# A planner that counts GpSimd's whole-tile operations as holding VectorE up

## The chip, the core and the metric

The kernel runs on one core of a Trainium2 chip. The metric is device time in microseconds of one execution; lower is better. The engines named below are TensorE (PE in the profile, with PEld for its weight loads), VectorE (DVE), ScalarE (ACT), GpSimd (POOL) and SyncE (SP), which issues every DMA of this kernel.

## What is computed

Three blocks in a row, all float32 (the inputs arrive as float64 where the code decodes them): a two-way attention between 512 tokens and 32 state rows for 8 batches and 8 heads, a feed-forward block with a SoLU and a layer norm, and a feed-forward block with a squared ReLU.

```python
scores = scale * np.matmul(x, state.transpose(0, 1, 3, 2))
a = softmax(scores);   xread = np.matmul(a, state)
a2 = softmax(scale * np.matmul(state, x.transpose(0, 1, 3, 2)));   sread = np.matmul(a2, x)
x = concatenate([xread, sread], axis=2)          # 4352 rows of 512
h = x @ w_in
solu = h * softmax(h);   ln = (solu - mu) / np.sqrt(var + 1e-06) * g_ln
x = ln @ w_out                                   # w_in 512x1024, w_out 1024x512
r = np.maximum(x @ w2_in, 0.0)
out = (r * r) @ w2_out                           # w2_in 512x2048, w2_out 2048x512
```

(`softmax` stands for the maximum, exponential and sum that the reference writes out.)

## The kernel before

Large products are made of three passes over a high half and a low half of each operand. ScalarE copies a tile into its high half, and a subtraction makes the low half; that subtraction can run on VectorE, or on GpSimd where both operands are in SBUF.

Phase one goes over 8 batches and a last group of 256 state rows. For each batch it computes scores (`scores`), transposes them (`emit_sT`, tile `sTp`), makes softmax weights `a_sb` and transposes these (`emit_aT`, tile `aTp`), multiplies state and `w_in` (`emit_sw`, tile `sw`), forms four tiles of `h` (`emit_l1`, PSUM tile `hps`), and takes each through `solu_rest`: maximum (L557, L574), exponential (L581), product (L586), square (L592), four small GpSimd operations for the root (L600 to L607), normalisation of `u` (L610). Then `emit_lnT` transposes `u` (tile `lnTp`), splits it into `lt` (ScalarE L653, VectorE L656), and `emit_l2` multiplies by `wo` into `y` (L682), which is stored in DRAM. The `h` of batch b+1 and the scores of batch b+2 are interleaved with the eight steps of batch b.

Weights are decoded on chip (`decode`: ScalarE L300, VectorE L303 and L306). `wi` and `wo` are decoded at the start. The weights of phase two's first product are decoded, combined and split in the background of batches 1 to 6 (`early_w2`, tiles `dec` and `w2s`, stored to DRAM as `w_d`), and those of its second product at the turn to phase two (`load_wb`, tiles `wb`). Phase two then goes over the nine groups with a seven-product scheme (`emit_l3`, L1005) and the last product (`emit_l4`, L1076).

TensorE's order is written out by hand. The order on all other engines is made by a planner in Python, class `Flow`, as the program is built; the chip then runs each engine's list in the order given, with semaphores. The planner keeps one clock `now`, and a time `free` for each of VectorE (V), ScalarE (A), GpSimd (P) and the DMA queue (D). Work off TensorE is written as generators that yield steps: a dictionary of engines with planned costs, a time from which the step is ready, and a function that emits it. Costs that matter here:

- the low half of a decoded weight tile (`split_w` and `keep` in `early_w2`): 1.25 on P or 0.69 on V;
- the softmax product in `rest` of `emit_sT` (L435): 1.2 on P or 0.69 on V;
- the normalisation of `u` (L610): 1.7 on P or 0.75 on V;
- the root of `solu_rest`: 2.4 on P, no choice.

`poll` goes over the open tasks by urgency (the due time found in a first planning round, less the costs still to come), takes a step if its chosen engine is free within 0.1 of `now`, and chooses the engine by the least of free time + cost + `SPARE`, where `SPARE` is 0.7 for V. `pe` moves the clock on by TensorE's planned times and marks due times. The program is planned twice: the second round takes due times and costs from the first.

```python
eng = min(engs, key=lambda e: max(self.free[e], self.now) + engs[e] + self.SPARE[e])
if self.free[eng] > self.now + self.EARLY:
    continue
```

Of the kernel before, what the change touches and what calls it, by code (L numbers as in the profile page):

```python
# [28 lines left out]
class Flow:  # L29
# [12 lines left out]

    SPARE = {"V": 0.7, "A": 0.0, "P": 0.0, "D": 0.0}
    NEVER = 1e9

    def __init__(self, plan=None):

        self.plan, self.made = plan, []
        self.now = 0.0
        self.end = 0.0  # L50
        self.warm = self.WARM_UP
        self.free = {"V": 0.0, "A": 0.0, "P": 0.0, "D": 0.0}
        self.tasks = []

    def run(self, eng, cost, ready, emit):
        start = max(self.free[eng], ready, self.now)
        self.free[eng] = start + cost
        emit(eng)
        return start + cost + (2.0 if eng == "D" else self.HOP)

    def spawn(self, gen, slack=8.0):


        task = {"gen": gen, "req": None, "done": None, "slack": slack, "costs": [],
                "by": self.NEVER, "n": len(self.made)}
        self.made.append(task)
# [36 lines left out]
    def latest(self, task):  # L103

        if self.plan:
            by, costs = self.plan[task["n"]]
            if by < self.NEVER:
                return by - sum(costs[len(task["costs"]):])
# [45 lines left out]
def attn_solu_relu2_kernel(  # L154
# [645 lines left out]
    def load_y(j):  # L800
# [7 lines left out]
        def few():  # L808
            for k in range(2):
                t, f = yield from raw_y(k)  # L810
                yield from split_y(j, k, t, f)
                give("raw")

        def gen():
            a1, f1 = yield from raw_y(0)
            a2, f2 = yield from raw_y(1)
            a11, a21, a12, a22 = (a[:, :, i:i + Q] for a in (a1, a2) for i in (0, Q))
            tmp = []
            yield from split_y(j, "A11", a11, f1)
            for _ in range(3):  # L820
                yield take("dec")
                tmp.append(dec_p.tile([P, 512], F32, tag="dec", name="sy", bufs=3).rearrange(
                    "p (k t) -> p k t", k=2
                ))
                if len(tmp) == 1:
                    s1 = tmp[0]
                    f2 = yield {"V": 0.69}, f2, lambda e: nc.vector.tensor_tensor(
                        out=s1, in0=a21, in1=a22, op=ALU.add
                    )
                elif len(tmp) == 2:  # L830
                    s2 = tmp[1]
                    f = yield {"V": 0.69}, f2 - fl.HOP, sub(s2, s1, a11)
                    yield from split_y(j, "S2", s2, f)
                    yield from split_y(j, "A12", a12, f2)
                else:
                    s3 = tmp[2]
                    f = yield {"V": 0.69}, f2, sub(s3, a11, a21)
                    yield from split_y(j, "S3", s3, f)
                    give("dec")
            yield from split_y(j, "S1", s1, f2)  # L840
            give("dec")
            f = yield {"V": 0.69}, f2, sub(s2, a12, s2)
            yield from split_y(j, "S4", s2, f)
            give("dec")
            yield from split_y(j, "A22", a22, f2)
            give("raw")
            give("raw")

        for name in range(2) if j == B else [a for _, a, _ in PRODUCTS]:
            done["y", j, name] = {"by": fl.NEVER, "done": None}  # L850
        done["y", j] = fl.spawn(few() if j == B else gen())
# [32 lines left out]
    for t in range(T):  # L884
        run(emit_l1(0, t, t % 2 == 0))
        if t % 2:
            emit_e(0, t // 2)
            if t < T - 1:
                exp_t(0, t // 2 + 1)
# [13 lines left out]
    for b in range(B):  # L903
# [5 lines left out]
        for k in range(K1):  # L909
# [28 lines left out]
            if b == B - 1:  # L938
                if k in (0, 2):
                    after[3].append(lambda: run(emit_l1s(k // 2)))  # L940
                if k == 3:
                    fl.need([done["w2_d", m] for m in range(M2)])
                    phase2_right()
                    load_y(0)
                if k in (4, 6):
                    load_wa(0, k // 2 - 2)
                if k in (5, 6, 7):
                    load_wb(wb_order[k - 5])
# [5 lines left out]
            if k in l1_at and nxt:  # L954
                run(emit_l1(b + 1, l1_at.index(k)))
# [203 lines left out]
```

## Time and profile before

| what | value |
|---|---|
| median of three runs | 1150.2 us (1149.54 to 1151.52) |
| profiled execution, its own time | 1151.89 us |
| its span, first to last instruction | 1149.7 us |
| TensorE busy | 1116.0 us (97%) |
| VectorE busy | 727.9 us (63%) |
| ScalarE busy | 457.5 us (40%) |
| GpSimd busy | 155.4 us (14%) |

The span leaves out what lies ahead of the first and behind the last instruction. Busy shares are means over stages that differ: GpSimd works in phase one and at the turn to phase two only, so a reader goes by stretches of the span and not by the shares of the whole. A group of instructions is named by line, engine, operation and tile; L256 is a helper's line that many subtractions share, and there the tile tells them apart.

### The profile page before, as it was taken

What the parts mean: (1) busy time and instruction counts of PE and PEld (TensorE: products, weight loads), DVE (VectorE), ACT (ScalarE), POOL (GpSimd) and SP (SyncE); (2) the same over time, 40 slices, a digit from 0 to 9 for tenths busy, and PEclk for the clock granted to TensorE, in tenths of its full rate; (3) what the DMA queues carried; (4) which work ended last, traced back from release to release, by engine and by line L of the source; (5) the groups of instructions that cost most, each with busy time, mean ns of one, the idle gap of its engine ahead of it and who ended that gap; (6) DMA issues with size and microseconds to landing.
All of it is one profiled execution on the core that took longest, in us unless ns stands there. A gap on an engine that the chain in (4) does not pass through costs nothing.

```text
span 1149.7 us, 17914 instructions
## 1 busy us (share of the span) xinstructions
PE 1116.0 (97%) x7144; PEld 943.9 (82%) x7144; DVE 727.9 (63%) x1429; ACT 457.5 (40%) x848; POOL 155.4 (14%) x209
## 2 busy tenths in 40 slices
PE   4899999999999999999999999999999999999998
PEld 1377777777777689999989999999899989989987
DVE  6776878778777468885655745745754655655522
ACT  5866767677766464331211221311211211221121
POOL 1532323334134122300000000000000000000000
PEclk8999999999999999999999999999999999999999
DMA  9322163462443729855555555556555565465353
GB/s 351 146 80 98 57 227 131 152 216 85 166 147 111 292 85 337 318 180 198 221 196 198 197 214 205 190 202 223 196 185 212 192 217 190 179 229 191 129 192 111
DMA packets 42691, 214.02 MB, mean 186 GB/s; under 512 B 4976, under 2 KB 14192, under 8 KB 31344
## 3 DMA queue, kind: packets, MB, share of 16 engines
q1 hardware_dynamic: 42608, 212.88, 51.6%
q8 instruction: 56, 0.92, 0.3%
q14 instruction: 27, 0.22, 0.1%
HBM read 178.26 MB, written 34.60 MB: 185 GB/s over the span
## 4 chain that ended last, share of the span: by engine, by line
PE 67%; DVE 1%; ACT 0%; DMA 0%; issue 0%; POOL 0%; SPq 0%; DVEq 0%; ACTq 0%
PE o L1076 32%; PE h L1005 30%; PE y L682 3%; PE hps L621 1%; DMA raw<-w_in 0%; PE lnTp L647 0%; DVE u L586 0%; DVE lt L656 0%; POOL wb L256 0%; DVE hm L557 0%; ACT e L581 0%; DVE u L610 0%; ACT u L250 0%; ACT lt L653 0%; DVE yt L256 0%
## 5 line engine op out<-in xcount | busy, mean ns | idle before, releaser
L1076 PE MATMUL o<-wb,g 128*128 128x512 f32 x1632 | 383.4, 390 | 0.0
L1005 PEld LDWEIGHTS h<-yt,wa 128*128 128x128 f32 x2880 | 354.9, 192 | 5.5
L1005 PE MATMUL h<-yt,wa 128*128 128x256 f32 x2880 | 356.6, 283 | 0.0
L1076 PEld LDWEIGHTS o<-wb,g 128*128 128x128 f32 x1632 | 301.9, 188 | 59.8
L682 PE MATMUL y<-lt,wo 128*128 128x512 f32 (+1 forms) x864 | 218.3, 394 | 3.1 <-ACT lt L653 2.4
L985 DVE TENSOR_TENSOR u<-u,h 128x256 f32<-128x256 f32 x192 | 80.3, 418 | 177.3 <-ACT u L250 151.6
L682 PEld LDWEIGHTS y<-lt,wo 128*128 128x128 f32 x864 | 148.9, 189 | 39.8 <-issue 5.9
L250 ACT CAST g<-r 128x512 fp32r<-128x512 f32 x136 | 82.5, 622 | 222.1 <-DVE r L993 222.1
L985 DVE TENSOR_TENSOR r<-u,h 128x256 f32<-128x256 f32 x256 | 100.7, 417 | 24.8 <-PE h L1005 24.7
L993 DVE SCALAR_TENSOR_TENSOR r<-r 128x512 f32<-128x512 f32 x136 | 89.6, 697 | 29.3 <-ACT r L1028 29.3
L621 PE MATMUL hps<-sw,aT 128*128 128x512 f32 x368 | 98.4, 416 | 1.0 <-ACT s_sb L356 1.0
L256 DVE TENSOR_TENSOR g<-r,g 128x512 fp32r<-128x512 f32 x136 | 88.3, 688 | 14.5 <-ACT g L250 11.2
L250 ACT COPY u<-h 128x256 f32<-128x256 f32 x64 | 23.8, 372 | 183.0 <-PE h L1005 183.0
L621 PEld LDWEIGHTS hps<-sw,aT 128*128 128x128 f32 x368 | 69.7, 192 | 24.8 <-issue 6.2
L656 DVE SCALAR_TENSOR_TENSOR lt<-lnTp,g_sb,lt 128x512 fp32r<-128x512 f32 (+1 forms) x72 | 51.4, 714 | 26.2 <-ACT lt L653 25.5
L557 DVE TENSOR_REDUCE hm<-hps 128x1 f32<-128x512 f32 x68 | 45.9, 687 | 26.6 <-PE hps L621 21.0
L250 ACT COPY u<-hps 128x512 f32<-128x512 f32 x68 | 39.1, 583 | 41.9 <-DVE hm L557 40.5
L653 ACT ACTIVATE lt<-lnTp,g_sb 128x512 fp32r<-128x512 f32 (+1 forms) x72 | 48.2, 671 | 5.4 <-PE lnTp L647 5.3
L586 DVE SCALAR_TENSOR_TENSOR u<-u,e 128x1024 f32<-128x1024 f32 x34 | 44.4, 1307 | 8.4 <-ACT e L581 8.2
L592 ACT ACTIVATE e<-u,nmu 128x1024 f32<-128x1024 f32 x34 | 39.2, 1153 | 12.7 <-DVE nmu L589 12.7
L647 PE MATMUL lnTp<-ident,u 128*128 128x128 f32 x272 | 41.6, 274 | 1.5 <-DVE a_sb L256 1.4
L581 ACT ACTIVATE e<-u,nmx 128x1024 f32<-128x1024 f32 x34 | 39.2, 1153 | 6.8 <-DVE nmx L574 5.8
(92 smaller groups left out, 838.4 us busy)
## 6 DMA issues: line engine op xcount, KB each, us to landing
wa<-w_d SPq DMA_DIRECT2D x64, 1792.0 KB, 7.2
w_d<-w2s SPq DMA_DIRECT2D x32, 512.0 KB, 2.9
raw<-w_out SPq DMA_DIRECT2D x24, 512.0 KB, 5.5
out<-osb SPq DMA_DIRECT2D x34, 256.0 KB, 4.9
xT<-x_t SPq DMA_DIRECT2D x8, 1024.0 KB, 5.2
xn<-x_n SPq DMA_DIRECT2D x8, 1024.0 KB, 6.7
y_d<-ys SPq DMA_DIRECT2D x16, 512.0 KB, 4.1
raw<-w_in SPq DMA_DIRECT2D x16, 512.0 KB, 5.9
```

Source lines behind the costliest of these rows:

```text
L250: nc.scalar.copy(out=out, in_=in_)
L256: return lambda e: eng_of[e].tensor_tensor(out=out, in0=in0, in1=in1, op=ALU.subtract)
L557: one({"V": 0.68}, lambda e, c=c, ps=ps: nc.vector.tensor_reduce(out=m2[:, c:c + 1], in_=ps, axis=AX.X, op=ALU.max)),
L586: nc.vector.scalar_tensor_tensor(out=u, in0=u, scalar=1.0, in1=e_, op0=ALU.mult, op1=ALU.mult, accum_out=us)
L621: nc.tensor.matmul(out=ps, lhsT=lhsT(i, k), rhs=rhs(j, k)[:, cs], start=(k == 0 and n == 0), stop=(k == n_k - 1 and n == len(passes) - 1),)
L653: f = yield {"A": 0.1 + nt * 0.143}, f, lambda e: nc.scalar.activation(out=o[:, 0], in_=pf, func=AF.Copy, scale=gk)
L656: f = yield {"V": 0.1 + nt * 0.155}, f, lambda e: nc.vector.scalar_tensor_tensor(out=o[:, 1], in0=pf, scalar=gk, in1=o[:, 0].bitcast(F32), ...
L682: nc.tensor.matmul(out=ps, lhsT=wo[k][:, w, c * P:(c + 1) * P], rhs=o[:, a], start=(k == 0 and i == 0), stop=(k == K1 - 1 and i == 2),)
L985: return then({"V": 0.42}, lambda e: nc.vector.tensor_tensor(out=out, in0=in0, in1=in1, op=op), *tasks)
L993: f = yield {"V": 0.69}, max(t["done"] for t in tasks), lambda e: nc.vector.scalar_tensor_tensor(out=r, in0=r, scalar=0.0, in1=r, op0=ALU. ...
L1005: nc.tensor.matmul(out=ps, lhsT=w[:, y, k], rhs=a[:, x, k], start=(first and k == 0 and i == 0), stop=(last and k == 1 and i == 2),)
L1076: nc.tensor.matmul(out=ops[j][t], lhsT=g[:, a, h, t * P:(t + 1) * P], rhs=wb[m + h * M2][:, w, :], start=(m == 0 and h == 1 and i == 0), s ...
```

## The change

`run`, which every planned step goes through, books VectorE as well when a step goes to GpSimd at a planned cost under 2.0: VectorE's free time becomes the later of itself and the step's start, plus 0.7 of the cost. The root (2.4) is left out by the bound. Nothing else is edited; the planner's lists of instructions follow from it.

```diff
     SPARE = {"V": 0.7, "A": 0.0, "P": 0.0, "D": 0.0}
     NEVER = 1e9
+    HELD = 0.7
...
     def run(self, eng, cost, ready, emit):
         start = max(self.free[eng], ready, self.now)
         self.free[eng] = start + cost
+        if eng == "P" and cost < 2.0:
+
+            self.free["V"] = max(self.free["V"], start) + self.HELD * cost
         emit(eng)
         return start + cost + (2.0 if eng == "D" else self.HOP)
```

## Rows read from the trace of the kernel before

**Rows 1.** Four stretches: from:to length, busy (instructions) by engine, granted clock, DMA share, GB/s.
```profile
0.00:18.80 18.80, 8.44 (x40) 2.22 (x40) 8.99 (x19) 8.48 (x13) 0.69 (x6) 0.99 0.91 332
18.80:60.00 41.20, 29.75 (x203) 13.83 (x203) 35.07 (x67) 33.67 (x67) 19.47 (x26) 0.83 0.52 195
60.00:424.00 364.00, 355.83 (x2353) 271.70 (x2352) 264.73 (x494) 245.90 (x459) 118.05 (x165) 0.99 0.41 145
424.00:1149.70 725.70, 721.99 (x4553) 656.15 (x4550) 419.07 (x852) 169.45 (x312) 17.19 (x13) 1.00 0.57 203
```

**Rows 2.** TensorE's waits: its line, who ended the wait, sum, times, longest.
```profile
PE aTp L462 <- POOL a_sb L435: 7.3, 2, 3.8
...
PE sTp L406 <- ACT s_sb L250: 3.3, 3, 1.8
...
PE lnTp L647 <- DVE a_sb L256: 1.4, 1, 1.4
...
PE sTp L406 <- DVE nmx L574: 1.2, 1, 1.2
...
PE sTp L406 <- DVE lt L656: 0.9, 1, 0.9
PE y L682 <- DVE lt L656: 0.5, 2, 0.3
PE srd L478 <- DVE aT L256: 0.2, 1, 0.2
```

**Rows 3.** GpSimd's groups: count | busy us, mean ns | idle before, releaser.
```profile
L610 POOL TENSOR_SCALAR u<-u,nmu,vs 128x1024 f32<-128x1024 f32 x20 | 27.3, 1366 | 2.1
L256 POOL TENSOR_TENSOR w2s<-dec,w2s 128x512 fp32r<-128x512 f32 x17 | 25.1, 1487 | 31.6 <-ACT w2s L250 31.6
...
L256 POOL TENSOR_TENSOR wb<-dec,wb 128x512 fp32r<-128x512 f32 x15 | 19.8, 1324 | 66.8 <-ACT wb L250 62.7 <-PE h L1005 4.1
...
L256 POOL TENSOR_TENSOR wo<-dec,wo 128x512 fp32r<-128x512 f32 x7 | 9.6, 1377 | 13.3 <-ACT wo L250 13.3
L435 POOL TENSOR_TENSOR a_sb<-a_sb,sm 128x512 f32<-128x512 f32 x8 | 8.7, 1082 | 25.3 <-DVE sm L432 25.3
```

**Rows 4.** VectorE's groups with SBUF operands, the same columns.
```profile
L586 DVE SCALAR_TENSOR_TENSOR u<-u,e 128x1024 f32<-128x1024 f32 x34 | 44.4, 1307 | 8.4 <-ACT e L581 8.2
L306 DVE SCALAR_TENSOR_TENSOR dec<-raw,dec 128x512 int32<-128x512 int32 x40 | 30.4, 763 | 0.8
...
L303 DVE TENSOR_SCALAR dec<-dec 128x512 int32<-128x512 int32 x40 | 20.2, 505 | 17.9 <-ACT dec L300 17.9
...
L256 DVE TENSOR_TENSOR w2s<-dec,w2s 128x512 fp32r<-128x512 f32 x15 | 13.1, 887 | 8.3 <-ACT w2s L250 8.2
...
L610 DVE TENSOR_SCALAR u<-u,nmu,vs 128x1024 f32<-128x1024 f32 x14 | 12.4, 886 | 1.8 <-POOL vs L607 1.8
```

**Rows 5.** Shortest/median/longest ns of groups, by tile or line; first and last start.
```profile
L303 DVE TENSOR_SCALAR dec<-dec x40: 411/420/1520, 25.3 to 484.0; 128x512 int32<-128x512 int32 x40
L306 DVE SCALAR_TENSOR_TENSOR dec<-raw,dec x40: 678/692/1711, 25.8 to 492.1; 128x512 int32<-128x512 int32 x40
...
L256 DVE TENSOR_TENSOR w2s<-dec,w2s x15: 677/690/1527, 144.6 to 382.6; 128x512 fp32r<-128x512 f32 x15
...
L586 DVE SCALAR_TENSOR_TENSOR u<-u,e x34: 1210/1224/2016, 37.2 to 402.6; 128x1024 f32<-128x1024 f32 x34
...
L557 DVE TENSOR_REDUCE hm<-hps x68: 679/684/694, 30.3 to 399.5; 128x1 f32<-128x512 f32 x68
```

**Rows 6.** Timeline near 54 us: start, length, instruction, [wait before and its releaser].
```profile
54.00 1.21 POOL L610 TENSOR_SCALAR u<-u,nmu,vs 128x1024 f32<-128x1024 f32 x1
...
54.34 1.40 DVE L610 TENSOR_SCALAR u<-u,nmu,vs 128x1024 f32<-128x1024 f32 x1
...
56.48 1.06 PE L647 MATMUL lnTp<-ident,u 128*128 128x128 f32 x8 [1.41 <-DVE a_sb L256]
```

**Rows 7.** Two stretches behind the waits at 223.79 and 270.28, columns as in 1.
```profile
222.00:228.00 6.00, 4.79 (x27) 3.87 (x26) 5.74 (x10) 4.46 (x10) 3.79 (x5) 1.00 0.43 175
270.00:276.00 6.00, 5.72 (x21) 4.62 (x22) 5.45 (x11) 3.41 (x7) 0.67 (x3) 0.72 0.01 1
```

## The prediction

> **What bounds the kernel now.** I read the stretches first, then TensorE's waits, then the groups of GpSimd and VectorE. The stretches [rows 1] split the span at the two points that matter here. The first whole-tile operation of GpSimd starts at 18.84 us, so nothing ahead of 18.8 us can change. After 424 us TensorE is busy 721.99 of 725.70 us, and the rest of that stretch is its end; phase two has no wait to give back. Between the two, TensorE is idle 41.20 - 29.75 = 11.45 us up to 60 us, and 364.00 - 355.83 = 8.17 us from there to 424 us. These 19.6 us, together with the clock of the early stretch (granted 0.83), are all that an order of the work can win. TensorE's program order is written out by hand and is not touched by the planner; the change can only move its waits.
>
> The waits [rows 2] say who ended them. The largest, 7.3 us in two pieces, is the start: TensorE waits for the softmax weights of batch 0. Waits ended by VectorE sum to 1.4 + 1.2 + 0.9 + 0.5 + 0.2 = 4.2 us. Those of `sTp` ended by ScalarE's copies are 3.3 us in three pieces, the longest 1.8. A wait for several semaphores is put down to the last one, so the 4.2 is a rough share and no exact one.
>
> **What the change books.** It touches one branch in `run`: any GpSimd step with a planned cost below 2.0 moves VectorE's free time to max(its free time, the start) + 0.7 of the cost. Three kinds qualify: the low halves at 1.25 (`wo`, `w2s`, `wb`), the softmax product at 1.2, and the normalisation of `u` at 1.7. The root at 2.4 does not. From GpSimd's groups [rows 3] there are 7 + 17 + 15 = 39 low halves, 8 products and 20 normalisations now: 39 x 0.875 + 8 x 0.84 + 20 x 1.19 = 34.1 + 6.7 + 23.8 = 64.6 us of VectorE time that the planner did not book before. No instruction is added, removed or made longer. What changes is where the steps stand in the lists of VectorE, ScalarE, GpSimd and SyncE, and on which engine the steps with a choice land.
>
> **How much of it is real.** The four largest groups with SBUF operands have means above their medians [rows 4, 5]: L306 763 against 692 ns (40 times, 2.8 us), L303 505 against 420 (40, 3.4 us), `w2s` 887 against 690 (15, 3.0 us), L586 1307 against 1224 (34, 2.8 us): 12.0 us together. Smaller groups may add as much again, so I put the real hold at 12 to 24 us, an estimate from these rows. The planner booked none of that and now books 64.6. The worst single ones are long (1520 ns for L303, 1711 for L306, 2016 for L586), so single delays of about 1 us are real and were missing in the plan. On the other side L557, which reads PSUM, lies between 679 and 694 ns in all 68 cases [rows 5], though GpSimd is busy 118.05 of 364 us in its stretch: such work isn't held at all, and the plan now holds it too.
>
> The Trainium skill, "SBUF — State Buffer", section "Who interferes with whom", says in my words that a VectorE instruction with two SBUF inputs contends with a GpSimd one that reads SBUF, and that one with at most one SBUF input outside the two-port modes does not. The trace agrees on L557. By that rule a hold of one size for every operation is wrong for much of VectorE's work, which speaks for the slower rival below.
>
> **What becomes of it, part by part.** *Choice of engine.* A step goes where free time + cost + spare is least, spare being 0.7 for VectorE. With both free, a low half takes GpSimd (1.25 against 0.69 + 0.7 = 1.39) and a normalisation takes VectorE (1.45 against 1.7). So what is on VectorE now went there because GpSimd was busy, for the low halves, or because it was not, for `u`. A later free time of VectorE moves some of the 15 `w2s` and 14 `u` [rows 4] to GpSimd. Price of one `u`: 1366 against 886 ns, +0.48 us to the tile's end; of one `w2s`, 1487 against 887, +0.60. VectorE loses the 0.9 us of work and takes a hold in place of it; by the rows the hold is between 0 and about 1 us, so the balance on VectorE is -0.9 to +0.1 us. I take it as nil for TensorE: VectorE is busy 264.73 of 364 us, and tiles of `u` are made one batch ahead. If that cover is gone, as at the start, the cost is the 0.48 or 0.60.
>
> *The start, 18.8 to 60 us.* The two products follow each other through one VectorE chain. VectorE is busy 35.07 of 41.2 us. Booking 0.84 us after each can put decode steps of `wi` ahead of the second chain or behind it. These are the same steps, all needed before the first large products, so I expect the sum to stand: 0, between -1 and +1 (one or two steps of 0.42 and 0.69, the medians of L303 and L306). Near 54 us [rows 6] two normalisations run at once, on GpSimd from 54.00 and on VectorE from 54.34 to 55.74; the transposes that read them start at 56.48, 0.74 us later. A booking of 1.19 us that puts one or two steps of 0.67 us ahead of the second costs between 0 and 1.34 - 0.74 = 0.6 us. Value taken: 0.
>
> *60 to 424 us.* Here the plan is too early on VectorE by the real hold, and now too late. A VectorE that looks busier starts fewer background steps (decoding, splitting `w2s`) ahead of the steps that TensorE waits for, and takes the most urgent when it comes free. That works on the waits that VectorE ended, at most 4.2 us. I take a third of it, -1.3 us, as only single waits among them stand near a held operation and most of VectorE's work here is not held at all. Covers: the `w2s` stores may come later, but they end at phase two's start and not at a wait of TensorE; the `wb` halves of phase two keep GpSimd as now (15 of 16), and the stretch after 424 us has no wait. Value taken there: 0; bounds 0 and +0.7, one step's length, for a half that comes late.
>
> **Sum.** -1.3 us. The profiled execution took 1151.89 us with a span of 1149.7, so 2.2 us lie outside the span; it is 1.7 above the median of 1150.2. The span's share goes to the same place in either, so I take the difference off the median: 1150.2 - 1.3 = 1148.9 us.
>
> **Rivals.** *Faster.* The order is truly better: all of the 4.2 us that VectorE ended goes, and nothing is late in its place: 1146.0. For it: delays of 1 us that the plan did not know. Against it: ScalarE's waits stand beside them, and next late may be its copies.
>
> *Slower.* The booking is three to five times the real hold, so VectorE's urgent PSUM steps (maxima, low halves of `lt`) are planned, and listed, too late, and ScalarE's list is built around these times. Place: the `sTp` transposes, once in each batch, where a PSUM bank must come free. A wait of 1.2 us there (at 223.79) left the clock at 1.00; the one of 1.8 (at 270.28) was followed by a stretch of 6 us granted 0.72 [rows 7], which is 0.28 x 6 = 1.7 us more. So if one wait of about 0.8 grows to the largest seen, it costs 1.0 + 1.7 = 2.7 us: 1150.2 + 2.7 = 1152.9. Two of them: 1155.6. It decides from the wait that the clock follows. Against it: due times still rank the steps.
>
> *No effect.* If the lists came out as they were, the program is the same: 1150.2. With 67 bookings this is unlikely, 0.02; it counts as same.
>
> **How the numbers follow.** A run of this kernel can tell about 0.2% from no change, 2.3 us, so same is 1147.9 to 1152.5. Forecast and no effect hold 0.43, the forecast's own range being that band. Faster has 0.33: the bookings are of the right kind and hit VectorE where it is busiest. Slower has 0.24. The range takes in the faster rival with half a microsecond beyond it, for luck at the start, and the slower one with a small part of its double: 1145.5 to 1154.0.
>
> **What would show it.** Right: TensorE busy as before, its waits after 60 us shorter by 1 or 2 us and those ended by VectorE most of all; more than 20 `u` and 17 `w2s` on GpSimd; the stretch after 424 us the same length within 1 us. The faster rival: no `sTp` wait over 1 us. The slower one: a second stretch with a low clock after 60 us. The forecast is wrong at its root if the stretch after 424 us or the first 18.8 us changes its length, or if the start moves by more than 2 us.

## The result, and the profile after

The change makes the kernel slower: 1158.9 us (1158.4 to 1160.1) against 1150.4 for the kernel before on the same chip, a ratio of 1.0075 (95% interval 1.0063 to 1.0087), or +8.5 us. The profiled execution of after has a span of 1158.3 us against 1149.7. Line numbers behind `run` are 4 higher than before.

The stretches of after, columns as in [rows 1]. The fourth is as long as the fourth of [rows 1]; it begins at 432.7 us, 0.9 us behind phase two's first product, where that of [rows 1] begins 4.9 us ahead of it. TensorE waits 0.1 us in those 4.9 us, so the idle times can be compared:

```profile
0.00:18.80 18.80, 8.60 (x40) 2.21 (x40) 8.85 (x19) 8.33 (x13) 0.68 (x6) 0.99 0.92 332
18.80:60.00 41.20, 30.13 (x204) 14.27 (x204) 33.55 (x65) 35.52 (x70) 23.04 (x27) 0.83 0.52 195
60.00:432.70 372.70, 361.55 (x2397) 277.31 (x2397) 253.93 (x482) 250.83 (x468) 136.00 (x183) 0.99 0.39 142
432.70:1158.30 725.60, 719.12 (x4506) 651.93 (x4505) 411.52 (x842) 165.43 (x303) 20.04 (x14) 1.00 0.57 202
```

The first 60 us look alike. TensorE is then idle 372.70 - 361.55 = 11.2 us up to phase two, against 8.2 in [rows 1], and 6.5 us behind it, against 3.7. Since TensorE's order is the same in both programs, its instructions can be laid side by side: the first `y` product starts at 59.12 us before and at 58.76 after (0.4 earlier), the last `lnTp` at 425.84 and 428.69 (2.9 later), a product `o` of phase two at 512.52 and 521.13 (8.6 later), and the end stays 8.6 later. So two places lose in this pair of traces: some 3.2 us between 59 and 429 us, and 5.7 us between 429 and 521 us.

TensorE's waits after, columns as in [rows 2]:

```profile
PE aTp L466 <- POOL a_sb L439: 7.4, 2, 3.9
...
PE xsp L515 <- ACT sr L500: 5.5, 3, 2.7
PE lnTp L651 <- DVE u L614: 3.8, 4, 1.3
PE sTp L410 <- ACT s_sb L254: 2.9, 3, 1.5
PE h L1009 <- ACT yt L254: 1.7, 1, 1.7
...
PE o L1080 <- POOL wb L260: 0.9, 1, 0.9
...
PE y L686 <- DVE lt L660: 0.8, 1, 0.8
...
PE ep L453 <- DVE a_sb L260: 0.6, 1, 0.6
PE sTp L410 <- DVE nmx L578: 0.6, 1, 0.6
PE h L1009 <- DVE yt L260: 0.2, 1, 0.2
```

The start's wait is the one of [rows 2]. New are two of the three waits of `xsp` (4.0 of the 5.5 us; the one of 2.0 before is 1.5 now), those of `lnTp` for the normalised `u`, and those in phase two, where the kernel before has none. The waits that VectorE ended sum to 3.8 + 0.8 + 0.6 + 0.6 + 0.2 = 6.0 us, against the 4.2 of [rows 2]. Between 60 us and phase two's first product they are 3.9 us, against 2.8, and those that ScalarE ended 6.9, against 5.2.

GpSimd's groups after, columns as in [rows 3]:

```profile
L614 POOL TENSOR_SCALAR u<-u,nmu,vs 128x1024 f32<-128x1024 f32 x22 | 33.4, 1516 | 2.0
L260 POOL TENSOR_TENSOR w2s<-dec,w2s 128x512 fp32r<-128x512 f32 x25 | 32.8, 1320 | 64.8 <-ACT w2s L254 64.8
L260 POOL TENSOR_TENSOR wb<-dec,wb 128x512 fp32r<-128x512 f32 x16 | 22.6, 1420 | 81.0 <-ACT wb L254 81.0
...
L439 POOL TENSOR_TENSOR a_sb<-a_sb,sm 128x512 f32<-128x512 f32 x16 | 17.4, 1088 | 53.6 <-DVE sm L436 52.1 <-ACT lt L657 1.5
...
L260 POOL TENSOR_TENSOR wo<-dec,wo 128x512 fp32r<-128x512 f32 x8 | 10.7, 1339 | 12.3 <-ACT wo L254 12.0
```

Of the steps with a choice, 20 went over: all 16 softmax products are on GpSimd (8 before), 25 `w2s` (17), 22 `u` (20), 16 `wb` and 8 `wo` (15 and 7). VectorE is busy 707.8 us in place of 727.9, and the kernel is slower all the same.

**Phase two.** Rows of after from its timeline (start, length, instruction, [wait before it and its releaser]):

```profile
468.93 0.33 SPq L236 DMA_DIRECT2D yraw<-y_d  x1
...
477.77 0.32 SPq L236 DMA_DIRECT2D yraw<-y_d  x1
...
489.54 0.33 SPq L236 DMA_DIRECT2D raw<-w_out  x1
...
490.21 1.63 POOL L260 TENSOR_TENSOR wb<-dec,wb 128x512 fp32r<-128x512 f32 x1 [8.59 <-ACT wb L254]
...
498.81 1.62 POOL L260 TENSOR_TENSOR wb<-dec,wb 128x512 fp32r<-128x512 f32 x1 [6.97 <-ACT wb L254]
...
505.84 1.27 POOL L260 TENSOR_TENSOR wb<-dec,wb 128x512 fp32r<-128x512 f32 x1 [5.40 <-ACT wb L254]
...
507.17 4.83 PE L1080 MATMUL o<-wb,g 128*128 128x512 f32 x20 [0.86 <-POOL wb L260]
509.74 0.66 ACT L304 ACTIVATE dec<-raw 128x512 f32<-128x512 f32 x1 [3.98 <-DMA raw<-w_out]
...
512.80 1.62 POOL L260 TENSOR_TENSOR wb<-dec,wb 128x512 fp32r<-128x512 f32 x1 [5.69 <-ACT wb L254]
514.45 0.69 DVE L260 TENSOR_TENSOR sy<-yraw 128x512 f32<-128x512 f32 x1 [1.18 <-POOL wb L260]
515.18 0.62 ACT L254 CAST yt<-sy 128x512 fp32r<-128x512 f32 x1 [2.45 <-DVE sy L260]
...
515.85 0.50 PE L1009 MATMUL h<-yt,wa 128*128 128x256 f32 x2 [1.70 <-ACT yt L254]
```

The two halves of the next group's `y` are fetched at 468.93 and 477.77 us, and each takes one of three `raw` buffers until the group is split. At that point four tiles of `wb` are still to come. They go one by one through the third buffer: low halves at 490, 499, 506 and 513 us, 7 to 9 us apart, ScalarE waiting for the transfer each time. TensorE waits 0.86 us for one; then VectorE's split of `y` waits for the `dec` tile that the last one frees, and TensorE waits 1.70 us for that. The clock falls behind this wait:

```profile
514.00:516.00 2.00, 0.30 (x3) 0.15 (x2) 0.86 (x2) 0.82 (x3) 0.42 (x1) 1.00 0.00 0
516.00:518.00 2.00, 1.78 (x9) 1.57 (x10) 2.00 (x5) 0.58 (x2) 0.00 (x0) 0.72 0.00 0
518.00:520.00 2.00, 2.00 (x9) 1.58 (x8) 1.98 (x5) 1.14 (x2) 0.00 (x0) 0.50 0.00 0
520.00:522.00 2.00, 2.00 (x14) 1.87 (x13) 1.39 (x5) 0.00 (x0) 0.00 (x0) 0.93 0.00 0
```

The granted share is the column before the DMA share: 0.28 + 0.50 + 0.07 of 2 us each are 1.7 us lost. With waits of 0.86, 1.70 and 0.22 that is 4.5 of the 5.7 us; the rest is not traced to a place. In the kernel before the second half of `y` was fetched at 481.93, with two `wb` tiles to come, and the last was there at 494.8, ahead of the product at 512.5:

```profile
468.97 0.33 SPq L232 DMA_DIRECT2D yraw<-y_d  x1
...
481.93 0.33 SPq L232 DMA_DIRECT2D yraw<-y_d  x1
...
482.59 1.30 POOL L256 TENSOR_TENSOR wb<-dec,wb 128x512 fp32r<-128x512 f32 x1 [1.74 <-ACT wb L250]
...
493.53 1.30 POOL L256 TENSOR_TENSOR wb<-dec,wb 128x512 fp32r<-128x512 f32 x1 [9.64 <-ACT wb L250]
494.87 0.69 DVE L256 TENSOR_TENSOR sy<-yraw 128x512 f32<-128x512 f32 x1 [1.73 <-POOL wb L256]
...
495.59 1.14 ACT L250 CAST yt<-sy 128x512 fp32r<-128x512 f32 x2 [2.13 <-DVE sy L256]
```

**Phase one.** The largest new wait there is at 298 us. Rows of after:

```profile
295.88 0.38 SPq L236 DMA_DIRECT2D w_d<-w2s  x1
297.12 0.62 ACT L254 CAST w2s<-dec 128x512 fp32r<-128x512 f32 x1 [3.95 <-DMA w_d<-w2s]
297.64 0.51 ACT L500 ACTIVATE sr<-srd,l 128x64 f32<-128x64 f32 x2
...
298.21 0.33 PE L515 MATMUL xsp<-ident,sr 128*128 128x128 f32 x1 [2.66 <-ACT sr L500]
```

`sr` is two short operations of ScalarE whose input was ready at 294.3 us. A background cast of `w2s` stands ahead of it in ScalarE's list and waits 3.95 us for a store to free its buffer. The wait at 160 us has the same form, behind a decode that waits 3.40 us for its load.

The clock falls behind the wait at 298 us as well:

```profile
298.00:304.00 6.00, 5.79 (x21) 4.66 (x22) 2.29 (x4) 1.83 (x5) 1.08 (x1) 0.72 1.00 356
```

In [rows 7] the same granted clock, 0.72 over 6 us, stands behind the wait of 1.8 us at 270 us. That wait and that stretch are gone in after, so between 63 us and phase two there is one such stretch in either trace, and only the one at 516 us comes on top.

### The profile page after: what moved, and what is told of

Read it like the earlier page. It is cut to its first block, busy times and chain, and to the rows that moved or that the text cites. A ratio compares the mean times of both kernels' runs of the same rounds, so it can differ in the third digit from the quotient of the medians.

```text
span 1158.3 us, 17925 instructions
## 1 busy us (share of the span) xinstructions
PE 1119.4 (97%) x7144; PEld 945.7 (82%) x7144; DVE 707.8 (61%) x1405; ACT 460.1 (40%) x852; POOL 179.8 (16%) x229
## 4 chain that ended last, share of the span: by engine, by line
PE 68%; DVE 3%; DMA 2%; issue 2%; POOL 1%; ACT 1%; POOLq 0%; SPq 0%; ACTq 0%; DVEq 0%
PE o L1080 31%; PE h L1009 29%; PE y L686 5%; PE hps L625 3%; DMA raw<-w_out 1%; DMA w_d<-w2s 1%; PE lnTp L651 1%; DMA raw<-w_in 1%; DVE lt L660 0%; DVE hm L561 0%; POOL wb L260 0%; POOL u L614 0%; DVE u L590 0%; ACT dec L304 0%; DVE dec L310 0%
## 5 line engine op out<-in xcount | busy, mean ns | idle before, releaser
L561 DVE TENSOR_REDUCE hm<-hps 128x1 f32<-128x512 f32 x68 | 46.2, 686 | 34.1 <-ACT u L254 20.4
L304 ACT ACTIVATE dec<-raw 128x512 f32<-128x512 f32 x40 | 26.9, 672 | 45.0 <-DMA raw<-w_out 26.0
L651 PEld LDWEIGHTS lnTp<-ident,u 128*128 128x128 f32 x272 | 33.1, 140 | 13.1 <-DVE u L614 5.1
```

Of the source, the lines that this page charges most:

```text
L561: one({"V": 0.68}, lambda e, c=c, ps=ps: nc.vector.tensor_reduce(out=m2[:, c:c + 1], in_=ps, axis=AX.X, op=ALU.max)),
L651: nc.tensor.transpose(ps[:, t, :], u_t[key, t][:, k * P:(k + 1) * P], ident)
```

## The experiments

All runs below are compared with the kernel before on the same chip in the same rounds; it spread there from 1148 to 1155 us, and the intervals of the ratios are 0.1 to 0.2% wide on either side. A place that is read from one trace is rougher. Before and e2 below have the same lists for every engine up to 420 us, and yet the products of e2 are 2.8 us earlier at 379 us: 1.9 us of it arose near 270 us, where e2 waits 1.5 us in place of 1.8 and its clock does not fall.

**The `wb` bookings, without and alone.** `split_w` gets its cost from `load_wb` under a type of its own (not shown here), and the branch asks for it:

```diff
-        if eng == "P" and cost < 2.0:
+        if eng == "P" and cost < 2.0 and not isinstance(cost, Wb):    # e1
+        if eng == "P" and isinstance(cost, Wb):                       # e2
```

> The changed kernel, but the 16 low halves of wb book nothing on VectorE; all other bookings stay. Theory T (the loss has two parts: some 2.9 us up to 429 us by the phase-one bookings, and 5.7 us between 507 and 521 us because the wb bookings push the decoding of the last wb tiles back): the second part goes, 1150.4 + 2.9 = 1153.3 us, and no wait for wb or yt in phase two. Rival R (the 5.7 us come from the late and changed state in which phase one hands over, not from the wb bookings): about 1158, waits at the first group of phase two as in the changed kernel.

> Only the 16 low halves of wb book VectorE (0.875 us each); phase one is planned as in the kernel before. Theory T: phase one as before (last lnTp at 425.8 us), then a wait for wb or for yt near 505 to 520 us, and 1150.4 + 5.7 = 1156.1 us, at least 1153. Rival R: 1150.4, no wait in phase two.

Without the `wb` bookings: 1.0040 (1.0025 to 1.0055), +4.6 us (2.9 expected), and no wait of TensorE for `wb` or `yt` in phase two; the waits of phase one are those of after (`xsp` 5.5 us, `lnTp` for `u` 3.8). With them alone: 1.0045 (1.0029 to 1.0060), +5.2 us, the lists of phase one as before, and in phase two (lines 4 higher than in after):

```profile
PE h L1013 <- ACT yt L258: 1.9, 2, 1.4
PE o L1084 <- POOL wb L264: 0.8, 1, 0.8
PE h L1013 <- DVE yt L264: 0.4, 2, 0.2
```

The two add to +9.8, the whole is +8.5; each is good to 1.4 to 1.8 us. So the loss has these two parts, and the second belongs to the `wb` bookings.

**A buffer for the next `y`.** From group 1 on the first half of `y` has a buffer of its own; all bookings stay:

```diff
+        raw = ["yraw" if j else "raw", "raw"]
...
-            yield take("raw")
-            t = raw_p.tile([P, 2, n], F32, tag="raw", name="yraw")
+            own = raw[k] == "yraw"
+            yield take(raw[k])
+            t = (p2["yraw"] if own else raw_p).tile([P, 2, n], F32, tag=raw[k], name="yraw")
...
```

> The changed kernel with all bookings, but from group 1 on the first half of the raw y has a buffer of its own, so that the y of group 1 takes one of the three raw buffers that the wb tiles are loaded through, not two. Theory T1 (what makes the last wb tiles late is that two of three raw buffers are held by y while four wb tiles are still to come, so that these come one by one, 7 to 9 us each): most of the 5.7 us go, 1153 to 1155 us, and the last four wb tiles come closer together. Rival T2 (VectorE's or the queue's list itself is late, buffers don't matter): 1158 to 1159.

1.0031 (1.0013 to 1.0049), +3.6 us. The last four `wb` halves come in pairs, at 489 and 499 us, and phase two has no wait. The last ends 71 us behind phase two's first product, against 83 in after and 66 before. So of the 17 us that it is late in after, some 12 go with the buffer, and the 5 that are left cost nothing.

**A booking too small to mean anything, and a stir of another kind.**

```diff
-    HELD = 0.7
+    HELD = 0.05        # e4
...
-    HOP = 0.12         # e10, in the kernel before
+    HOP = 0.125
```

> HELD is 0.05 in place of 0.7: a booking of 0.06 to 0.085 us, too small to stand for any hold. It shows how far the time moves when the lists are only stirred. Theory T (the loss is due to the size of the bookings): within 1.5 us of 1150.4. Rival S (any stir of the lists moves the time by several us, whatever is booked): 1153 to 1160, with waits of TensorE at other places than before.

> The kernel before with no booking at all; the planner's allowance between two engines is 0.125 in place of 0.12, a stir that stands for nothing. Theory of size: within 1.5 us of before. Rival S: 0 to 8 us slower.

e4: 1.0002 (0.9990 to 1.0013), no change. e10: 1.0019 (1.0010 to 1.0028), +2.2 us, from waits at other places (1.4 us for ScalarE's copy of `u` at 167 us, `sTp` 1.2 us at 181). e4 fits its theory; e10 is above the 1.5 us of its own. The two stirs tried cost 0 and 2.2 us, well under 8.5; two do not say how far others would go.

**One kind of booking at a time, phase one.** The branch asks for a cost of 1.7 (`u`), 1.2 (softmax products), or 1.25 without `wb` (`wo`, `w2s`):

```diff
-        if eng == "P" and cost < 2.0:
+        if eng == "P" and cost == 1.7:                                   # e5
+        if eng == "P" and cost == 1.2:                                   # e6
+        if eng == "P" and cost == 1.25 and not isinstance(cost, Wb):     # e7
```

> Only the normalisations of u (planned at 1.7 on GpSimd, 1.19 us booked) hold VectorE in the plan. Theory U (the waits of lnTp for u that the changed kernel has, 0.4 to 1.3 us each, come from normalisations on VectorE that are listed 1.2 us late): lnTp waits of 2 to 4 us in all for VectorE's u, no xsp wait after 60 us; 2 to 4 us slower than before. Rival S (the parts have no place of their own, phase one is a new draw of the order with each setting): waits at any place, between 2 us faster and 4 us slower.

> Only the softmax products (1.2 on GpSimd, 0.84 us booked, 16 of them at most) hold VectorE. Theory: they are few and their tiles are due much later, so within 1 us of before, the start (up to 60 us) within 1 us too. Rival S: between 2 us faster and 4 us slower, waits at any place.

> Only the low halves of wo and w2s (1.25 on GpSimd, 0.875 us booked, 25 to 33 of them) hold VectorE; wb does not. Theory W (the two xsp waits of the changed kernel, 1.3 and 2.7 us, come from a background step of ScalarE, decode or w2s, that stands ahead of sr in its list and waits for a DMA; the background work is what the w2s bookings push late): xsp waits of about 4 us in all after 60 us, no lnTp waits for u; 3 to 5 us slower than before. Rival S: no such wait, between 2 us faster and 3 us slower.

e5: 0.9997 (0.9986 to 1.0007), no change. e6: 1.0063 (1.0049 to 1.0077), +7.2 us. e7: 1.0029 (1.0017 to 1.0040), +3.3 us. The theories of e5 and e6 fell, e6 beyond its rival's 4 us too; that of e7 has the size that it named but not the waits. `u` alone brings no more than 0.4 us of `lnTp` waits for VectorE's `u`; the softmax products, of which I expected nothing, cost most; and `w2s` alone brings no `xsp` wait after 60 us. e6 and e7 lose 3 to 4 us ahead of 70 us, where the whole change loses nothing: in e6 `srd` waits 3.1 us for ScalarE's copy of `ep` (1.4 before), and `lnTp` 1.8 us for GpSimd's `u`. -0.3, +7.2 and +3.3 do not add to the +4.6 of e1. So the loss of phase one can't be shared out among the kinds.

**The size of the booking.** HELD 0.25, 0.35 and 0.5 for all kinds, and 0.35 with the stir of e10.

```diff
-    HELD = 0.7
+    HELD = 0.35        # e9; e13: 0.25; e14: 0.5; e15: 0.35 with HOP = 0.125
```

> HELD is 0.35, half of the change, for every kind. Theory of size (the loss grows with the booking): 3 to 5 us slower than before, with some of the delay of the last wb tiles. Rival S (each setting is a new draw of the order, and the order of the kernel before is a good draw): anywhere between no change and 8 us slower, with waits at places of its own.

> HELD is 0.25, about the share of GpSimd's whole-tile time by which VectorE's work is longer in the traces. Theory of size: 2 to 4 us faster than before, no wait for wb or yt in phase two. Rival S: anywhere between 4 us faster and 8 us slower.

> HELD is 0.5. Theory of size: between the results at 0.35 (3.8 us faster) and 0.7 (8.5 slower), so 0 to 5 us slower than before, the last wb tile between the 497 us of 0.35 and the 513 us of 0.7. Rival S: outside of that, with no order in where the last wb tile stands.

> HELD 0.35 with the allowance between engines at 0.125 in place of 0.12, the stir that cost 2.2 us without a booking. Theory of size: the gain outlives the stir, 1.5 to 4 us faster than before. Rival S: the gain is a draw and goes, 0 to 6 us slower than before.

0.25: 0.9976 (0.9967 to 0.9985), -2.8 us. 0.35: 0.9967 (0.9955 to 0.9978), -3.8 us. 0.35 with the stir: 0.9977 (0.9968 to 0.9986), -2.6 us. 0.5: 1.0140 (1.0124 to 1.0157), +16 us. Theory and rival of e9 both fell, as neither had a gain; e13 and e15 came out by their theories, but for a wait of 0.2 us for `yt` in e13; e14 by its rival. The gain is there for two sizes and outlives the stir, but not at the same place: at 70 us the products of e9 are 1.8 us ahead of before's and those of e15 1.1 us behind. The loss at 0.5, larger than at 0.7, speaks against a smooth course: the products of e14 are 3.2 us ahead of before's at 400 us and 16.6 behind at 450. The longest of e14's waits, two of its three pieces at the turn, and its timeline there:

```profile
PE y L686 <- ACT lt L657: 11.5, 3, 7.1
```

```profile
404.43 1.64 ACT L254 CAST w2s<-dec 128x512 fp32r<-128x512 f32 x3
...
409.92 0.62 ACT L254 CAST w2s<-dec 128x512 fp32r<-128x512 f32 x1 [3.85 <-DMA w_d<-w2s]
410.44 0.68 ACT L657 ACTIVATE lt<-lnTp,g_sb 128x512 fp32r<-128x512 f32 x1
...
411.18 2.07 PE L686 MATMUL y<-lt,wo 128*128 128x512 f32 x4 [7.06 <-ACT lt L657]
```

The last of the background `w2s` is still under way at the turn to phase two, where the planner stops until it is done; ScalarE's list has its casts, one blocked 3.85 us by a store, ahead of `lt`. In the kernel before the same cast, held 3.09 us by its store, stood beside 7.0 us of products that wait for nothing:

```profile
379.17 7.03 PE L621 MATMUL hps<-wi,xs 128*128 128x512 f32 x16
...
381.97 0.62 ACT L250 CAST w2s<-dec 128x512 fp32r<-128x512 f32 x1 [3.09 <-DMA w_d<-w2s]
```

**A longer landing time in the plan.** Loads of weights are planned to land 3.4 us after issue and take 5.5 to 6.9 in the median in the traces of before and after:

```diff
-        return start + cost + (2.0 if eng == "D" else self.HOP)
+        return start + cost + (4.5 if eng == "D" else self.HOP)     # e11: after; e12: before; e16: HELD 0.35
```

> The changed kernel, with 4.5 us in place of 2.0 in the plan from the end of a DMA's share of the queue to its landing (512 KB from weights: planned 1.4 + 2.0, traced 5.5 to 6.9). Theory W (sr is late because a background step of ScalarE that waits for a DMA is planned ahead of it, the DMA being planned as landed): no xsp wait on sr between 100 and 350 us, 2 to 5 us faster than the changed kernel, so 1 to 6 us slower than before. Rival: the xsp waits stay or are replaced by as much elsewhere.

> The kernel before, with the same 4.5 us to landing and no booking. Theory of truth (a plan nearer to the chip gives a better order): 1 to 4 us faster than before. Rival S (a new draw): 0 to 8 us slower.

> HELD 0.35 and 4.5 us to a DMA's landing in the plan; alone they gave 3.8 and 3.0 us. Theory of truth (both corrections bring the plan nearer to the chip): 4 to 7 us faster than before. Rival S: they don't add, between 3 us faster and 20 us slower, as the landing time did on the changed kernel.

e12: 0.9974 (0.9963 to 0.9985), -3.0 us. e16: 1.0055 (1.0041 to 1.0070), +6.3 us. e11: 1.0209 (1.0194 to 1.0224), +24 us. In e11 the later `xsp` waits are gone (one of 1.5 us is left, at the start), as expected; but `y` waits 13.3 us for `lt`, and in e16 8.6 us, again at the turn. The times of e11 and e16 are outside their theories (1 to 6 us slower, 4 to 7 faster); e12 is inside. The two corrections of e16 each help alone and do not add: with both, the background work reaches the turn too late, as the table below shows.

**A hold on SBUF steps alone.** The flat booking is replaced: GpSimd's whole-tile steps and VectorE's steps with SBUF operands exclude each other in the plan, and steps on PSUM aren't held. One of the marked steps is shown:

```diff
+        if (eng == "P" and cost < 2.0) or isinstance(cost, Held):
+            start = max(start, self.lock)
+            self.lock = start + (1.25 if eng == "P" else cost)
         self.free[eng] = start + cost
...
-        f = yield {"V": 0.46}, f, lambda e: nc.vector.tensor_scalar(
+        f = yield {"V": Held(0.46)}, f, lambda e: nc.vector.tensor_scalar(
```

> The flat booking is replaced: GpSimd's whole-tile steps (for 1.25 us) and VectorE's steps with SBUF operands (decode, low halves from SBUF, L586, u, squares) exclude each other in the plan, and steps that read PSUM are not held. Theory (the size of the booking is what hurts; a hold of the right size and kind does not push the wb tiles late): no wait for wb or yt in phase two, and within 2 us of before, or up to 3 us faster. Rival (any hold in the plan makes the last wb tiles late): waits at wb or yt near 505 to 520 us, 3 to 6 us slower.

1.0039 (1.0027 to 1.0052), +4.5 us, with `xsp` waiting 3.9 us (1.9 of it at the start) and `lnTp` 1.8 for `u`, and 0.8 us in phase two for `yt`. My theory named no more than 2 us; it fell. The plan now leaves steps on PSUM free, as L557 is in [rows 5], but with 69 whole tiles at 1.25 us it books over 80 us of full exclusion, far more than the 20 us in sum that the trace of before shows (below). So this run does not say what a hold of the right kind and size would do.

**Where each run loses.** From one trace of each kernel, TensorE's products laid beside those of before. The first mark is the `hps` product that starts at 379.17 us before, the second is phase two's first product. "At the first mark" is how much later a run is there than before (earlier where negative); "turn" is what it loses from there to the second mark, and "phase two" what it loses behind that. Beside these stand the end of the last low half of `w2s`, counted from the first mark, and that of `wb`, counted from the second.

| kernel | change, us | at the first mark, us | last `w2s`, us | turn, us | last `wb`, us | phase two, us |
|---|---|---|---|---|---|---|
| before | 0 | 0 | 4 | 0 | 66 | 0 |
| stir alone (e10) | +2.2 | +1.1 | 4 | 0.0 | 66 | 0.3 |
| 0.05 (e4) | +0.2 | -1.9 | 4 | 0.0 | 57 | 0.5 |
| 0.25 (e13) | -2.8 | -9.0 | 27 | 4.4 | 75 | 1.0 |
| 0.35 (e9) | -3.8 | -2.3 | 15 | -0.3 | 73 | 0.0 |
| 0.35 and stir (e15) | -2.6 | -1.2 | 15 | -0.3 | 73 | 0.0 |
| 0.5 (e14) | +16 | -3.2 | 36 | 15.6 | 77 | 4.2 |
| 0.7 (after) | +8.5 | +2.0 | 16 | 0.8 | 83 | 5.8 |
| 0.7 without `wb` (e1) | +4.6 | +1.1 | 17 | 1.0 | 65 | 0.5 |
| 0.7, `wb` alone (e2) | +5.2 | -2.8 | 4 | -0.3 | 82 | 5.2 |
| 0.7, buffer for `y` (e3) | +3.6 | +0.8 | 17 | 0.9 | 71 | 0.4 |
| 0.7, `u` alone (e5) | -0.3 | -5.1 | 26 | 2.6 | 68 | 1.5 |
| 0.7, products alone (e6) | +7.2 | +4.5 | 4 | 0.0 | 65 | 0.6 |
| 0.7, `wo`, `w2s` alone (e7) | +3.3 | +2.5 | 4 | 0.0 | 67 | 1.3 |
| SBUF steps alone (e8) | +4.5 | +1.0 | 16 | 0.3 | 78 | 1.9 |
| landing 4.5 (e12) | -3.0 | -5.0 | 16 | -0.8 | 80 | 2.0 |
| 0.35, landing 4.5 (e16) | +6.3 | -10.8 | 36 | 13.7 | 80 | 2.8 |
| 0.7, landing 4.5 (e11) | +24 | -4.1 | 41 | 19.3 | 87 | 9.6 |

The turn costs 1 us at most with the last `w2s` by 17 us behind the mark, 2.6 and 4.4 us at 26 and 27, and 14 us and more from 36 on. Phase two loses 1.5 us at most with the last `wb` by 75 us, 1.9 to 4.2 at 77 to 80 (the 4.2 of e14 with a wait of 2.1 for `g`), and 5.2 and more from 82 on. Background work can be 12 us later and cost 1 us or nothing, and then falls off an edge. Phase one has its own draw beside these edges: e6 loses its time there and at neither edge, and e13 and e16 are 9 and 11 us ahead at the mark and give half of it or more back at the turn. As two traces with the same lists differ by 2.8 us there, a few us in that column mean little.

## Why the prediction was wrong, point by point

*Phase two, "value taken there: 0; bounds 0 and +0.7".* This is the step that failed first: 5.7 us in the trace, 5.2 with those bookings alone. I had asked whether `wb` would change engine (it doesn't, 15 and then 16 of 16) and whether that stretch had a wait (none, [rows 1]). Neither says how late a tile may come. Sixteen bookings of 0.875 are 14 us, put on an engine that was busy 18.06 of 20 us between 460 and 480 us; counted from phase two's first product the last half then ended at 83 us in place of 66, 16.7 us later. The room can be read from the trace of before. The last half was there at 494.8 us and its product began at 512.5: 17.7 us, enough by itself. But the split of the next `y` waits for the `dec` tile of that half (494.87 in the rows); its cast ended near 496.2 us and its product stood at 509.64, which leaves 13.4 us. And the half before the last was there at 483.9 and needed at 502.95: 19.1 us, where it came 20.4 us later by the same count. These are the two places at which after waits. I had read none of the three. "No wait" is not "room".

*60 to 424 us, -1.3.* It came out at about +3.2 in the trace and, by the median times, +4.6 without the `wb` bookings (e1). The step that failed is that a VectorE which looks busier delays background steps and so shortens the waits that VectorE ends. The base was wrong already: of the 4.2 us, 1.4 stand at 56.48 us [rows 6], ahead of this stretch, so 2.8 were left. And they did not shrink, they grew from 2.8 to 3.9 us, for `u` above all, which I had put at nil for a cover of one batch. The new `lnTp` waits (0.4 to 1.3 us), which come at the first transposes of a batch, show that the last tile of `u` of a batch does not have that cover. The waits ended by ScalarE grew from 5.2 to 6.9 us: its list runs in order, and a background cast that waits for a DMA holds it, and with it `sr` (2.66 us at 298). Which booking does which is not shown, as the kinds do not add.

*The start, 0.* Right for the whole change, 0.4 us earlier at 59 us. That it was luck is seen in e6 and e7, which lose 3 to 4 us by 70 us with part of the same bookings; my bounds of -1 and +1 were too narrow for reorderings.

*The booking against the real hold.* 64.6 us against 12 to 24 really held: the second figure holds for the trace of before. Taking for each VectorE group the median of the operations that no whole-tile GpSimd operation overlaps as its own length, those overlapped were 20 us longer in sum before, 0.22 of GpSimd's 91 us of whole-tile work. A booking near that, 0.25 and 0.35, is faster; 0.7 is not. I had both numbers and took from them a faster kernel for 0.7, a sign that fits 0.25 and 0.35.

*The slower rival.* Its cause, a booking three to five times the hold that makes work late, is what e2 shows for phase two; its place was not right. I had named `sTp` and the clock there; phase two loses by the background work, at its last due times. That made the range end at 1154.0. Its sign, a second stretch with a low clock after 60 us, did come, at 516 us. So did the sign that the forecast is wrong at its root: phase two is 5.7 us longer. The sign of the faster rival, no `sTp` wait over 1 us, did not: one of 1.5 us is left.

*Choice of engine.* More than 20 `u` and 17 `w2s` on GpSimd: 22 and 25. Right, and without worth.

What stays open: why phase one loses, and why its parts do not add. Each is a new order of some 560 VectorE and 550 ScalarE instructions up to 430 us; the stir of e10 shows 2.2 us from that alone, and no run here separates what of e1's +4.6 is more than that. Nor is the hold's size shown to be the cause of the gain at 0.25 and 0.35: three settings agree, but they gain at different places, and e12 gains as much with no booking at all.

## What to carry to other kernels

A wrong cost in a planner acts where work has a last due time and shares buffers: look there for the room, in microseconds, of every tile and of what waits behind it for the same buffer, before calling a stretch without waits safe. Try a planner's constant at several sizes, the one that the trace gives in sum first (here 0.22 of GpSimd's time), and beside an idle stir; two good corrections together can pass an edge that neither reaches alone. Of the versions tried, HELD 0.35 is the fastest, 3.8 us ahead of the kernel before; the intervals of 0.25, of 0.35 with the stir and of e12 overlap with its own.

## What the runs showed of the hardware that I had not expected

VectorE's delay did not grow with GpSimd's work: after moves 20 more whole tiles to GpSimd, and VectorE's overlapped operations are then longer by 14 us in sum, not more than the 20 before (0.12 of 117 us of whole-tile work, against 0.22 of 91). GpSimd's own whole tiles got longer in part: counted over the shortest of each group, 12.0 us in sum against 8.6. Its normalisations of `u` take 1516 ns on average in place of 1366 (1197 at the shortest in both, 2522 at the longest in after), its `w2s` halves 1320 in place of 1487. What decides which of the two engines is held is not shown by these runs.
